# RetNet attention and a SwiGLU block on one core: the first pair in chunks of 128, the sixth weight asked for later, and three more seven-product sets in tile two

## The chip, the core and the metric

The kernel runs on one core of a Trainium2 chip. The metric is device time in microseconds. The engines are TensorE (PE, with its weight loads shown apart as PEld), VectorE (DVE), ScalarE (ACT), GpSimd (POOL) and SyncE (SP, which here only issues transfers). ACT issues transfers too, on a queue of its own, and POOL a few.

## The reference

```python
# attention: q, k, v are (8, 8, 576, 64), float32
scores = q @ k^T / 8
gamma  = 1 - 2**(-5 - head)                       # one decay for each head
ret    = scores * gamma**(i - j)  where i >= j, else 0
x      = (ret @ v), heads side by side            # (8*576 tokens, 512)
# SwiGLU block, weights float64 in DRAM
g   = x @ w_gate                                  # 512 -> 1536
out = (silu(g) * (x @ w_val)) @ w_out             # 1536 -> 512
```

## The kernel before

**Attention** goes by pairs of heads: pair `i` is batch `i // 4`, heads `2p` and `2p + 1` of it, 32 pairs in all. It is computed in chunks: within a chunk scores are masked with a triangle of decays (`near`), across chunks a state of 64x64 a head is carried on. For a pair, `transposes` turns q and k so that head positions lie on partitions (the first four pairs on PE, against the identity, later ones on DVE), `keys` scales the keys for the states, `scores` and `new_states` are matmuls of 64x64, `masked` is the mask and the chain of state sums on DVE (`own`, `pairs`, `odd`, `evens`), `own_values` and `earlier_values` are the matmuls with v and with the states, and `to_x` writes the result into the activations `x`, which lie with features on partitions. One attention step, `tick(t)`, does the values of pair `t - 2`, the scores and states of pair `t - 1` and the transposes of pair `t`. Its DVE and ACT parts go into a list, `pieces`, and are issued a few at a time between other work (`part_on`, `go_on`).

**The weights** are float64 in DRAM, so each has 1 MB pieces (18 of them, in `order`), loaded by `load_w(m)` into three raw buffers and a fourth place, and turned into float32 in halves of 512 columns: `split(j)` on ACT (two instructions, L389 and L390) and `rounding(j)` on DVE (L406 and L407). When a second half has been split, the load of the next weight into the freed place is issued: from the sixth weight on (`m >= 5`) on ACT's queue, else on SP's. The load of the sixth weight is not issued there but put into a list, `held`, and taken out later.

**The tokens** are 4608. Tile one has 512 and is multiplied plainly: `up0(f)` is block `f` of 128 hidden features, gate and value, over four chunks `c` of 128 input features, then SiLU on ACT and the product on DVE; `down0` follows. While it runs, PE also works off attention pairs 4 to 11. The other four tiles have 1024 tokens each and use two nested levels of a seven-product scheme (Strassen's) in the up projection, and a 26-product scheme in the down projection (`down_step`).

**The up stage** of a 1024-token tile goes over 3 blocks of hidden features (`qd`) by 7 outer products (`SETS`, in the order 1, 2, 6, 7, 4, 5, 3). Each of these 21 sets is done either by seven inner products, which need sums of x blocks (`x_inner`, on POOL) and sums of weights (`w_inner`, on POOL), or plainly, as eight: `PLAIN` lists the plain ones, all in tile two (`n == 1`), where the sums are still being made. A slot is one product: two matmuls of 256 columns at L1186. A product is read out of its bank by DVE (`combine`, L1042) or ACT; four banks go round. A plain set reads each bank once for its two slots (set 5 twice), a set of seven reads each product. `finish` is SiLU on ACT (L1200) and a product on DVE or POOL (L1201).

In tile two the weight sums are made on POOL, used, and stored to DRAM (`store`, on SP) for the later tiles. `later(at, f)` puts an instruction ahead of slot `at`; `begins[k]` is the first slot of set `k`.

**Order.** From L1425 on the order on every engine is as written in the code. Before it the loads are issued in this order: on SP the small tables (`tab`, 64 columns), then pair by pair q, k, v, pairs 0 to 3, the large tables between pairs 2 and 3, then the weights; pairs 0 and 1 have one head on SP's queue and one on ACT's. Then `tick(0)` to `tick(5)` do pairs 0 to 3, with the first weights and the first blocks of `up0` between them; then `plan` runs the rest of tile one.

Of the kernel before, what the change touches and what calls it, by code (L numbers as in the profile page):

```python
# [22 lines left out]
def tables(gamma, scale, L):  # L23
# [15 lines left out]
             both(g[:, None] ** L), both(g[:, None] ** (2 * L)), pieces, runs, both(scale * g[:, None] ** at),  # L39
# [70 lines left out]
PLAIN = {(1, qd, o) for qd in range(3) for o in (1, 2, 4, 5, 3) if qd == 0 and o == 1 or o in (4, 5, 3)}  # L110
# [21 lines left out]
def kernel(  # L132
# [121 lines left out]
    def load(i):  # L254
# [6 lines left out]
        if i < HP:  # L261
# [11 lines left out]
            for h in heads:  # L273
                queues[i % 2].dma_start(out=blocks(t)[:, h % 2], in_=v[b, h, 0:CW].rearrange("(c p) d -> p c d", p=P))
# [35 lines left out]
    NCOL = 6 * H + 4 * HP  # L310
    nc.sync.dma_start(out=tab[:, 0:NCOL], in_=decays[:, 0:NCOL])
    load(0)
    load(1)
    ident = const.tile([P, P], F32, name="ident")
    make_identity(nc, ident)
    nc.scalar.activation(out=io[:, 0:1], in_=ident[:, 0:1], func=AF.Silu)
    inv, key = tab[:, 0:H], tab[:, H : 2 * H]
    step = tab[:, 2 * H : 2 * H + 2 * HP]
    piece = tab[:, 2 * H + 2 * HP : 2 * H + 4 * HP]
    run = tab[:, 2 * H + 4 * HP : NCOL]  # L320
# [11 lines left out]
    even_heads, odd_heads = slice(0, H, 2), slice(1, H, 2)  # L332
    for rows in half:
        decay(slice(0, H), slice(0, H), rows)

    load(2)
    nc.sync.dma_start(out=tab[:, NCOL:], in_=decays[:, NCOL:])
    load(3)
# [20 lines left out]
    def load_w(m, parts=range(2)):  # L359
# [8 lines left out]
        if i < NUP:  # L368
            for cols in [ts(2 * f + n, D) for f in parts for n in range(2)] if m <= RAWS else [slice(0, 2 * P)]:
                queue.dma_start(out=dst[:, :, cols], in_=src[:, :, cols])  # L370
        else:
            queue.dma_start(out=dst.rearrange("p (f c) n -> p f (c n)", f=2), in_=src)
# [38 lines left out]
    for f in range(2):  # L411
        for m in range(2):
            load_w(m, (f,))
# [30 lines left out]
    def vector(i):  # L444

        return i == 0

    def transposes(i):
# [6 lines left out]
        copy = nc.scalar.copy if i else nc.vector.tensor_copy  # L455
        if i < HP:

            mine = (bankC, bankE) if i + 1 == HP else (bankB, bankA)
            parts = [(kT, kn, mine[0]), (qT, qk, mine[1])]
            if i == 0:  # L460
                parts.reverse()

            def turn(t, src, bank):
                for c in range(NFULL):
                    to = bank[:, c : 4 * P : NFULL] if t is qT and scaled(i) else bank[:, ts(c, P)]
                    nc.tensor.transpose(to, src[:, ts(c, P)], ident)

            def put(t, _, bank):
                if i or t is qT:
                    copy(t[:, 0:CW], bank)  # L470
                else:
                    copy(t[:, 0 : CW // 2], bank[:, 0 : CW // 2])
                    nc.scalar.copy(t[:, CW // 2 : CW], bank[:, CW // 2 :])

            if i + 1 == HP:
                for part in parts:
                    turn(*part)
                pieces = [lambda part=part: put(*part) for part in parts]
            else:
                for part in parts:  # L480
                    turn(*part)
                    put(*part)
# [13 lines left out]
        def keys():  # L496
# [5 lines left out]
            for hl, rows, at in parts:  # L502
                scale = key[rows, 2 * p + hl : 2 * p + hl + 1]
                if vector(i) or 1 < i < HP:
                    (nc.vector if vector(i) else nc.gpsimd).tensor_scalar(out=at, in0=at, scalar1=scale, scalar2=None, op0=ALU.mult)
# [5 lines left out]
        return [keys] + pieces  # L511
# [64 lines left out]
    def masked(i):  # L576
# [6 lines left out]
        def copies():  # L583
            (nc.vector.tensor_copy if vector(i + 1) else nc.scalar.copy)(out=even, in_=z[:, 0])
# [151 lines left out]

    def tick(t, lo=HP, hi=NP, spread=False, then=None):
        go_on(len(pieces))
        if hi == HP:

            def new_pair():
                scores(t - 1, True)
# [827 lines left out]
```

## Time and profile before

| | |
|---|---|
| median of three runs | 1018.75 us (1016.43 to 1019.09) |
| profiled execution | 1014.55 us, of which the span 1012.8 |
| PE | 1000.9 us busy, 99% of the span |
| DVE | 710.9 us, 70% |
| POOL | 561.8 us, 55% |
| ACT | 286.7 us, 28% |
| DMA | 194.38 MB, mean 192 GB/s |
| first matmul | 4.63 us after the span's start |
| first matmul of `up0` | 24.11 us |
| tile two's up stage | 172.2 to 319.4 us |

The profile is of one execution. Its times count from the span's start. "Busy" for PE is the time in which a matmul is under way; matmuls overlap, so the distance from start to start tells more than a duration. A group of PE with "x4" counts records: a float32 matmul has two of them, a transpose one. "A <- B" in a list of waits says that A was idle and that B's end released it.

### The profile page before, as it was taken

To read this page: it belongs to the slowest core of one execution; us is meant where nothing else is said; L and a number is where in the kernel's file an instruction comes from. 1 tells how busy PE (TensorE), PEld (TensorE's weight loads), DVE (VectorE), ACT (ScalarE), POOL (GpSimd) and SP (SyncE) were. 2 spreads that over 40 slices of the span, in tenths; PEclk is the share of its full clock that TensorE was granted. 3 is DMA by queue.
4 is the path that set the end of the run, shared out by engine and by line. 5 is a ranking of instruction groups with operands and counts; after the bars stand their busy time and mean duration, and the time that the engine had idled before them with its cause. 6 is when DMAs were issued, how large, how long until landed. Compare 5 with 4: busy or idle time off the path is not lost.

```text
span 1012.8 us, 21319 instructions
## 1 busy us (share of the span) xinstructions
PE 1000.9 (99%) x8336; PEld 825.5 (82%) x8336; DVE 710.9 (70%) x1206; ACT 286.7 (28%) x636; POOL 561.8 (55%) x589
## 2 busy tenths in 40 slices
PE   6999999999999999999999999999999999999998
PEld 5655555888888888888888888888888888888887
DVE  4488887677875766977777678866575767566645
ACT  4565522132423312133422202233220012232110
POOL 3400359979375228575564157746672586566514
PEclk9999999999999999999999999999999999999999
DMA  9999866967587787647677777434454554445553
GB/s 245 261 288 272 192 216 234 264 193 214 138 238 207 217 231 193 198 156 196 184 202 206 198 179 217 154 133 159 161 172 141 154 189 147 148 155 180 182 159 102
DMA packets 278892, 194.38 MB, mean 192 GB/s; under 512 B 212552, under 2 KB 246088, under 8 KB 278792
## 3 DMA queue, kind: packets, MB, share of 16 engines
q1 hardware_dynamic: 251464, 94.70, 36.7%
q10 hardware_dynamic: 26688, 97.92, 29.1%
q8 instruction: 66, 1.08, 0.5%
q0 software_dynamic: 640, 0.39, 0.2%
q14 instruction: 34, 0.28, 0.1%
HBM read 154.04 MB, written 38.93 MB: 191 GB/s over the span
## 4 chain that ended last, share of the span: by engine, by line
PE 94%; DVE 2%; DMA 1%; POOL 1%; SPq 0%; issue 0%; ACT 0%; DVEq 0%; ACTq 0%; POOLq 0%
PE bankB L1186 12%; PE bankC L1186 11%; PE bankA L1186 11%; PE bankE L1186 11%; PE bankB L1392 7%; PE bankC L1392 7%; PE bankE L1392 6%; PE bankA L1392 6%; PE outer L532 2%; PE bankE L853 2%; PE bankA L853 2%; PE outer L1186 2%; PE inner L1186 2%; PE bankB L853 2%; PE outer L559 2%; PE bankC L853 2%
## 5 line engine op out<-in xcount | busy, mean ns | idle before, releaser
L1042 POOL TENSOR_TENSOR rest<-rest 128x512 f32<-128x512 f32 (+1 forms) x139 | 148.0, 1076 | 159.9 <-DVE rest L1042 112.5
L1201 POOL TENSOR_TENSOR arena<-rest,io 128x256 f32<-128x256 f32 x168 | 123.9, 750 | 89.4 <-ACT io L1200 88.9
L1200 ACT ACTIVATE io<-rest 128x256 f32<-128x256 f32 x192 | 79.3, 417 | 200.0 <-DVE rest L1042 140.0
L1186 PE MATMUL bankB<-rest,arena 128*128 128x256 f32 x448 | 114.5, 380 | 0.0
L1042 DVE TENSOR_TENSOR rest<-bankB,rest 128x512 f32<-128x512 f32 x116 | 78.5, 685 | 40.5 <-PE bankB L1186 28.5
L1186 PE MATMUL bankC<-rest,arena 128*128 128x256 f32 x416 | 106.3, 380 | 0.0
L1186 PE MATMUL bankA<-rest,arena 128*128 128x256 f32 x412 | 104.8, 379 | 0.0
L1042 DVE TENSOR_TENSOR rest<-bankA,rest 128x512 f32<-128x512 f32 x111 | 75.2, 685 | 40.8 <-PE bankA L1186 19.3
L1042 DVE TENSOR_TENSOR rest<-bankC,rest 128x512 f32<-128x512 f32 x110 | 74.5, 683 | 38.0 <-PE bankC L1186 23.4
L1042 DVE TENSOR_TENSOR rest<-bankE,rest 128x512 f32<-128x512 f32 x106 | 71.7, 684 | 36.2 <-PE bankE L1186 17.6
L1186 PE MATMUL bankE<-rest,arena 128*128 128x256 f32 x372 | 94.9, 380 | 0.3 <-DVE rest L1042 0.3
L1186 PEld LDWEIGHTS bankB<-rest,arena 128*128 128x128 f32 x448 | 84.7, 190 | 11.9 <-DVE rest L1042 0.2
L1186 PEld LDWEIGHTS bankC<-rest,arena 128*128 128x128 f32 x416 | 78.5, 190 | 11.4 <-DVE rest L1042 0.8
L1186 PEld LDWEIGHTS bankA<-rest,arena 128*128 128x128 f32 x412 | 78.1, 190 | 10.9 <-DVE rest L1042 0.2
L1186 PEld LDWEIGHTS bankE<-rest,arena 128*128 128x128 f32 x372 | 70.3, 190 | 10.4 <-DVE rest L1042 0.8
L1042 POOL TENSOR_TENSOR arena<-arena 128x256 f32<-128x256 f32 (+1 forms) x76 | 70.3, 947 | 11.1 <-PE bankC L1186 9.0
L886 POOL TENSOR_TENSOR rest<-rest 128x512 f32<-128x512 f32 x21 | 28.5, 1377 | 72.1 <-DVE rest L407 58.5
L1392 PE MATMUL bankB<-arena 128*128 128x256 f32 x264 | 61.0, 381 | 0.0
L1392 PE MATMUL bankE<-arena 128*128 128x256 f32 x264 | 60.8, 380 | 0.0
L1392 PEld LDWEIGHTS bankE<-arena 128*128 128x128 f32 x264 | 50.0, 190 | 6.9
L1392 PEld LDWEIGHTS bankB<-arena 128*128 128x128 f32 x264 | 49.8, 190 | 6.9
L1392 PE MATMUL bankC<-arena 128*128 128x256 f32 x240 | 55.2, 379 | 0.0
(270 smaller groups left out, 1876.0 us busy)
## 6 DMA issues: line engine op xcount, KB each, us to landing
arena<-up ACTq DMA_DIRECT2D x63, 896.0 KB, 4.6
arena<-dn ACTq DMA_DIRECT2D x65, 384.0 KB, 3.1
arena<-dn SPq DMA_DIRECT2D x39, 384.0 KB, 3.1
out_dram<-rest SPq DMA_DIRECT2D x31, 256.0 KB, 3.4
qk<-in_q_dram SPq DMA_DIRECT2D x108, 72.0 KB, 3.1
qk<-in_k_dram SPq DMA_DIRECT2D x108, 72.0 KB, 3.4
dn<-rest SPq DMA_DIRECT2D x26, 256.0 KB, 2.8
up<-arena SPq DMA_DIRECT2D x13, 512.0 KB, 5.6
```

The lines of the kernel that those rows point to most:

```text
L532: m = nc.tensor.matmul(value(i, hl, c), s["v"][rows, at], ret[rows, c % 2 if whole(i) else hl, c // 2], start=start, stop=start, skip_grou ...
L559: nc.tensor.matmul(xr[half[hl]] if c + 1 == NC else value(i, hl, c), state[half[hl], c, :], s["qT"][half[hl], ts(c, L)], start=False, stop ...
L853: nc.tensor.matmul(bank, w, xs[0][:, c, :], start=(c == 0), stop=(c == HP - 1))
L886: eng.tensor_tensor(out=dst, in0=srcs[0], in1=srcs[1], op=ALU.add if op[0] == "add" else ALU.subtract)
L1042: eng.tensor_tensor(out=out, in0=a, in1=b, op=ALU.add if sign > 0 else ALU.subtract)
L1186: m = nc.tensor.matmul(b[:, g * TB : (g + 1) * TB], w[:, g], x, start=(opens and g == 0), stop=True, skip_group_check=True)
L1200: nc.scalar.activation(out=s, in_=src[:, 0:TB], func=AF.Silu)
L1201: (nc.vector if busy and o != 2 and qd + 1 < NQ else nc.gpsimd).tensor_tensor(out=hid[:, qd, 2 * H + h, 2 * T + t], in0=src[:, TB : 2 * TB ...
L1392: nc.tensor.matmul(b[:, m * TB : (m + 1) * TB], lhs[:, qd, ts(m, P)], w[:, qd], start=(opens and qd == 0 and m == 0), stop=(qd == NQ - 1), ...
```

## The change

1. **Loads.** q and k of pairs 0 and 1 are asked for first, their v after them (`load` now returns a function that asks for v). The small tables grow by 132 columns to 196 and go behind the first head's k. Pair 2 follows, then the first halves of weights 0 and 1, pair 3, the other halves, and weights 2 and 3, these in one transfer each instead of four. The large tables go behind the load of pair 4.
2. **Pair 0** is done in chunks of 128 tokens (`first_scores`, `first_states`, `first_own`, `first_out`), with tables of its own, and q is scaled as it is copied out of its bank. Matmuls whose result is not used are put in front of and between its transposes.
3. **The start** is written out step by step instead of by `tick`. Weight halves are rounded, and parts of `up0(0)` done, between pairs 1, 2 and 3.
4. **The sixth weight.** `held` is worked off after `to_x(3)` instead of before `split(4)`.
5. **Pair 4's first attention step** goes behind `up0(2)`.
6. **Three sets** of tile two, (1, 3), (2, 4) and (2, 3) as (`qd`, set), are no longer in `PLAIN`. The x sums of sets 3 and 4 are made on POOL for them, into places of their own.
7. **Attention steps in tile two**: five in the up stage, at slots 56, 70, 84, 97 and 111, and five in the down stage at steps 1, 5, 10, 14 and 19. Before there were six, spread evenly from slot 56 on, and four. Three fetches of down operands are asked for 36, 39 and 43 slots after the third block's start, instead of 36, 38 and 40.

```diff
-PLAIN = {(1, qd, o) for qd in range(3) for o in (1, 2, 4, 5, 3) if qd == 0 and o == 1 or o in (4, 5, 3)}
+PLAIN = {(1, qd, o) for qd in range(3) for o in (1, 2, 4, 5, 3) if qd == 0 and o == 1 or o in (4, 5, 3)} - {(1, 1, 3), (1, 2, 4), (1, 2, 3)}
...
-            for cols in [ts(2 * f + n, D) for f in parts for n in range(2)] if m <= RAWS else [slice(0, 2 * P)]:
+            for cols in [ts(2 * f + n, D) for f in parts for n in range(2)] if m < 2 else [slice(0, 2 * P)]:
...
-    for f in range(2):
-        for m in range(2):
-            load_w(m, (f,))
+    for m in range(2):
+        load_w(m, (0,))
+    load(3)()
+    for m in range(2):
+        load_w(m, (1,))
     load_w(2)
     load_w(3)
...
+    def first_scores():
...
+        for _ in range(2):
+            nc.tensor.matmul(bankB[0:D, 0:D], ident[0:D, 0:D], ident[0:D, 0:D], start=True, stop=True)
+        for src, bank, idle in ((None, None, 6), (qk, bankE, 2), (kn, bankC, 1)):
+            for c in range(NFULL if bank else 0):
+                nc.tensor.transpose(bank[:, ts(c, P)], src[:, ts(c, P)], ident)
+            for _ in range(idle):
+                nc.tensor.matmul(bankB[:, 0:P], ident, ident, start=True, stop=True)
...
+        for c, hl in first:
+            nc.tensor.matmul(inner[:, hl, ts(c, P)], kT[half[hl], ts(c, P)], qT[half[hl], ts(c, P)],
+                             start=True, stop=True, skip_group_check=True)
...
+        if n == 1:
+            new[4] = [w_up[:, NQ - 1, 0, h, k, :] for h, k in ((0, 0), (1, 0), (0, 1))]
+            new[3] = [xs[2][:, h, TW - TB :] for h in range(3)]
...
-            for o, at in {7: 6, 1: 22}.items():
+            second, third = begins[len(SETS)], begins[2 * len(SETS)]
+            for o, at in {7: 6, 1: 22, 3: second + 38, 4: third + 17}.items():
...
-    for t in range(HP + 2):
-        tick(t, 0, HP)
-
-        if t == 3:
-            load(HP)
-        for j in {3: (1,), 5: (4, 5)}.get(t, ()):
-            rounding(j)
+    scale_run(1)
+    first_scores()
+    scale_run(2)
+    turn_pair(1)
+    first_states()
+    first_own()
+    new_pair(1)
+    turn_pair(2)
+    first_out()
+    split(0)
+    rounding(0, False)
+    scale_run(3)
+    new_pair(2)
+    own_values(1)
+    split(1)
...
+    up0(0, [0], [0])
+    earlier_values(1)
+    to_x(1)[0]()
+    put = transposes(3)
+    rounding(1, False)
+    for f in put:
+        f()
+    up0(0, [1], [0])
+    up0(0, [0], [1])
+    split(2)
+    own_values(2)
+    earlier_values(2)
+    up0(0, [1], [1])
+    to_x(2)[0]()
+    rounding(2)
+    rounding(3, False)
+    new_pair(3)
+    load(HP)
+    nc.sync.dma_start(out=tab[:, NCOL:], in_=decays[:, NCOL:])
+    split(4)
+    up0(1, range(2))
+    own_values(3)
+    earlier_values(3)
+    to_x(3)[0]()
+    while held:
+        held.pop()()
+    rounding(4)
+    rounding(5, False)
     for c in range(2, HP):
         for f in range(2):
             up0(f, [c])
+    split(6)
     load(HP + 1)
```

## The prediction

> **What bounds the kernel now.** I read the page's engine totals first, then TensorE's waits, the chain that ended last, and the timeline of the first 40 us and of tile two.
>
> ```profile
> PE 1000.9 (99%) x8336; PEld 825.5 (82%) x8336; DVE 710.9 (70%) x1206; ACT 286.7 (28%) x636; POOL 561.8 (55%) x589
> ```
>
> Of the 1012.8 us span TensorE (PE) idles 11.9. Its waits show where:
>
> ```profile
> PE bankA L466 <- DMA qk<-in_q_dram: 4.6, 1, 4.6
> PE outer L532 <- ACT rest L389: 1.0, 1, 1.0
> PE inner L573 <- ACT rest L470: 0.7, 1, 0.7
> PE inner L573 <- DVE kT L472: 0.5, 1, 0.5
> PE bankE L1186 <- DVE rest L1042: 0.3, 1, 0.3
> ```
>
> All but 0.3 or so lie before 34 us; from there PE runs without a gap to the end. So two things shorten this kernel: reaching that gapless run earlier, and having fewer matmuls in it. "Busy" hides a third loss, in PE's timeline (start, us, line, count):
>
> ```profile
> 9.67 1.12 PE L466 MATMUL bankB<-ident,kn 128*128 128x128 f32 x4
> 12.36 1.13 PE L573 MATMUL inner<-rest,kT 64*64 64x64 f32 x32 [0.72 <-ACT rest L470]
> 20.54 0.66 PE L466 MATMUL bankC<-ident,rest 128*128 128x128 f32 x4
> 27.74 0.69 PE L573 MATMUL inner<-rest,kT 64*64 64x64 f32 x32
> ```
>
> Four transposes take 0.90 from start to next start at 9.67 and 0.49 at 20.54; 32 score records 0.90 and 0.51. The rate doubles at 17.0, though the granted clock reads 1.00 in every stretch. Last, the chain up to the gapless run:
>
> ```profile
> 27.81 0.62 PE inner L573 x32
> 28.43 0.53 PE inner L543 x32
> ...
> 29.39 0.69 DVE rest L580
> 30.08 0.40 DVE rest L596
> 30.50 0.30 DVE rest L603
> ...
> 31.60 0.40 DVE rest L608
> ...
> 33.37 0.68 PE outer L559 x28
> 34.05 1.05 PE bankA L853 x2
> ```
>
> It is pair 3's scores, mask and states, then its last values, then the first matmul of chunk 2 of `up0`, at 34.05. Ahead of it DMA moves 220 to 340 GB/s from 2 us on without a pause, so the order of the loads matters.
>
> **The start, step by step.** I lay the new order out with the durations of these rows. By the ends of their packets in the trace, q of pair 0 lands at 4.6, k at 5.9, pair 2 by 13.1, pair 3 by 17.0, the halves of weights 0 and 1 at 18.9, 20.8, 22.8, 24.7 (1.9 each, 0.52 MB). In the new order the second table part (0.26 MB) leaves this stretch, the first grows by 0.07, and pair 3 (0.79 MB, 3 us) goes behind two halves: halves at 15.2 and 17.1, pair 3 at 20.1, the other two halves at 22.1 and 24.0, weight 2 at 27.8, weight 3 at 31 (estimates).
> - To 7.7: nothing is won. PE still waits for q (4.4) and k (5.7). The larger table is asked for third and lands near 6.5; DVE's product of q (0.69), the kT halves (0.42, 0.37) give scores at 7.7, before 7.62. The nine 128-column filler matmuls and two small ones take about 0.43 each at the slow rate (one of 256 columns takes 0.43 at the fast one), in time PE would wait; at most the one behind k's transposes costs 0.4.
> - Pair 0 by 128: scores 8 matmuls (0.85: 8 x half of 0.43, two side by side), states 8 (0.43), own 8 (0.85), earlier 6 (0.64), 2.8 where 64-token chunks take 2.4 fast but cost about 3.6 at the slow rate.
> - Pair 1: transposes to 10.1 (its q lands 7.2, POOL's L735, 1.04, ends 9.65 behind both `near` selects), ACT copies 0.6 each to 10.95, keys 0.9 to 11.85, states done 12.65 (before 15.1); its DVE mask and states (2.5) to 15.65.
> - `split(0)` on ACT waits for the half at 15.2, two at 0.6: 16.4; `rounding(0)` on DVE ends 17.05; the first `up0` matmul starts there, before 24.11.
> - Pair 2's mask and states queue behind it on DVE to 19.6, `rounding(1)` to 20.7. PE waits in order for pair 3's k (19.3), then two `up0` matmuls and pair 2's values to 23.2.
> - `split(2)` at 22.1 ends 23.4, the x copies 24.5, `split(3)` 25.7, `rounding(3)` 26.4, then pair 3's chain as above (2.3) to 28.7, values 0.65: chunk 2 starts at 29.4 to 29.9, before 34.05. **Minus 4.4** (middle). This end is set by DMA (22.1), then ACT and DVE in turn.
>
> The rate is the weak step. Before, PE was busy from 12.36 to 17.0 without a gap and then turned fast; after, fillers keep it busy from about 1.6 (ident is made by 1.5) to scores; 1.6 + 4.6 is 6.2, and with the gap at 4.3 I take it as fast by 8.5. The Trainium skill, "TensorE: Matmul & The Clock Gate", Part 1, says the array starts at half clock and is released by one free-running window of about 3.4 us of sustained work; the trace agrees with a turn after 4.6 us of it. The same page's Part 4 says transposes don't count as busy for this gate; here they do appear inside the 4.6 us (15.12 to 17.0), so the trace neither confirms nor clearly breaks it; by it the sum would be that of the first rival.
>
> **Weights and loads after it.** Weight 4 goes ahead of pair 4's load on SP: it landed at 48.3 (ACT waited 4.4 for it), now about 35. The sixth weight is asked for at about 30, as now (29.64, issue 0.41 on ACT), so about 4 us late against PE; it lands at about 39 (8.0 as now). `split(10)` on ACT waits for it, with the SiLU of block 2 queued behind; PE needs that bank at 51. Cost 0; without that cover, what it is later than 51. Weights 2 and 3 go as one issue instead of four: SP's issue time (3.1 and 4.1), hidden by transfers. Table part two, behind pair 4's load, is first read at 72.6. Pair 4's first attention step moves behind `up0(2)`: its transposes (1.5 on DVE) are needed by pair 4's states at 50 (54.9 now), load landed at about 43. Cost 0, covered by about 5 us.
>
> **Three sets.** A plain set is 8 slots, a seven-product set 7. A slot is two matmuls of 256 columns; the timeline has them 0.863 apart (218.81, 219.67, 220.54). 3 x 0.863 = **minus 2.6**, if nothing stalls:
> - DVE reads 7 products instead of 4 banks: 9 reads more, 0.60 from start to start, 5.4 us.
> - POOL gets eight sums of 128x256 (0.73): 5.8 us.
> - Attention step 17 (2.25 on PE, 4.0 on DVE) goes from the up stage to the down stage, PE time unchanged; DVE was 3.8 busy of 10 at 320. The others stand closer, 14 slots.
>
> DVE is the tight one:
>
> ```profile
> 240.00:250.00 10.00, 10.00 (x49) 8.79 (x48) 9.58 (x19) 0.99 (x3) 9.02 (x14) 1.00 0.57 198
> 260.00:270.00 10.00, 10.00 (x173) 8.75 (x171) 9.93 (x20) 4.37 (x10) 4.71 (x5) 1.00 0.13 22
> ```
>
> (columns: PE, PEld, DVE, ACT, POOL, clock, DMA). Slots 97 to 111 are the worst: 11 reads 6.6, eight products with SiLU at 0.34 2.7, one attention step with what is left over 4.7: 14.0 of 14 slots and one step on PE, 14.3. It fits, and a product may be read up to four slots late (3.4) before its bank is written again. POOL idles 9.0 at 256, where set 3's sums go (needed at 261), and for set 4 has 8 us of work against about 11. I take 0.3 for small stalls, as the one of 0.2 at 274. From 0 to 2.6 is open. The three later fetches go with the ring; they stood 9 us before use, now 7.
>
> **Sum.** -4.4 - 2.6 + 0.3 = -6.7. The profiled execution is 1014.55 (span 1012.8 and 1.75 around it), 4.2 below the median of the three runs (1018.75), so: 1007.9 for such a run, 1012.0 for a median.
>
> **Rivals.**
> 1. PE stays at the slow rate until about 14.6 (chance 0.13). Up to pair 1's states it then spends 0.85 + 0.9 + 0.43 + 0.85 + 0.8 more, less 0.9 of idle: 2.9, passed down the chain. -3.8: 1014.9. For: gaps at 4.3 and transposes among the fillers. Against: the turn at 17.0.
> 2. DMA keeps its pace and PE, 4 us ahead, waits for it between 45 and 75 (0.12): start gain given back, 1016.2. For: DMA share about 1.0 up to 110, k of pairs 5 and 6 landing (54.4, 72.4) only 5 to 7 us before their transposes. Against: SP has pauses waiting for buffers (73.7 to 77.2), so DMA can catch up, and weights are split 15 us before use.
> 3. Slower: DVE becomes the bound in tile two (0.07). Once it is over four slots late, each of its microseconds is PE's: the 5.4 of reads and steps 15 and 16 brought forward (8.0) make 13.4, so +6.7: 1025.5. For: 9.93 of 10 at 260. Against: the count above, and 2.6 idle at 252.
> 4. The sets don't give what they say, since sums come late on POOL and each set waits a slot (0.08): 1014.4.
>
> **Numbers.** My forecast has 0.60. About 0.3% (3.1 us) is what a measurement can tell. Below 1015.7: the forecast, rival 4, most of rival 1, a little of the spread of 2: 0.79. Within: the rest of 1, most of 2: 0.13. Above 1021.8: rival 3 and what I overlooked: 0.08. The range goes from 1008 (start -5.5, sets -2.6, and a run lower by the 2 that the three runs spread) to 1017 (rivals 1, 2, 4 in).
>
> **What would show it.** First `up0` at about 17 instead of 24.1 and chunk 2 near 29.6; transposes of pair 1 at 0.11 each; PE gapless after; 154 slots instead of 157 in tile two with the same 0.863; POOL's sums of set 3 before 261. It is wrong if PE waits for L389, L406 or loads between 30 and 75, if L1186 waits on DVE L1042 for over 1 us in total, or if chunk 2 starts later than 32.

## Result and the profile after

The changed kernel takes **1031.57 us** (median of four runs, 1029.3 to 1034.7) where the one before takes 1018.25 (1016.43 to 1019.09): ratio **1.0142**, interval 1.0117 to 1.0167. It is slower by 13; forecast were 1012.0 and a range that ended at 1017. The profiled execution took 1034.70, with a span of 1033.0, against 1014.55 and 1012.8 before. The spans differ by 20.2, and the readings below are made against that. The profile after is the slowest of its four executions and the one before is faster than all four beside it, so some 7 of the 20.2 us may be the spread between executions. Below, line 869 of the changed kernel is L853 of the one before, L1205 is L1186, L1058 is L1042, L1412 is L1392, L872 is L856.

The engine totals of the page after:

```profile
PE 1007.7 (98%) x8294; PEld 829.9 (80%) x8294; DVE 723.8 (70%) x1213; ACT 286.0 (28%) x636; POOL 566.5 (55%) x598
```

PE has 42 records fewer, and is busy 6.8 us longer. Its idle time is 25.3 (span less busy) where it was 11.9. The list of its waits after (us in total, times, longest):

```profile
PE bankB L1412 <- DMA arena<-dn: 5.8, 1, 5.8
PE bankA L869 <- ACT io L872: 4.8, 2, 3.6
PE bankA L1205 <- DVE rest L1058: 2.9, 1, 2.9
PE inner L558 <- issue: 2.0, 1, 2.0
PE bankB L732 <- POOL ident masks.py:199: 1.6, 1, 1.6
PE outer L552 <- DVE kT L477: 1.3, 1, 1.3
PE bankA L869 <- DVE arena L416: 0.9, 1, 0.9
```

Of the first four, only 0.3 at L1186 was there before. All but the fifth and the last stand behind 70 us, in three places: ahead of 130, near 275, near 405 (the last, at 18.39, is the first `up0` matmul). Why busy time grew although matmuls were taken out shows in the windows around the three long waits (PE, PEld, DVE, ACT, POOL, granted clock, DMA share, GB/s):

```profile
100.00:110.00 10.00, 6.42 (x13) 2.45 (x12) 6.50 (x13) 8.44 (x16) 0.00 (x0) 0.88 1.03 264
110.00:120.00 10.00, 10.00 (x154) 5.50 (x153) 8.53 (x17) 7.27 (x15) 1.37 (x1) 0.95 0.89 214
270.00:280.00 10.00, 6.17 (x56) 5.11 (x57) 7.75 (x14) 2.32 (x7) 2.88 (x3) 0.91 0.78 166
280.00:290.00 10.00, 10.00 (x119) 8.52 (x121) 8.27 (x17) 4.39 (x10) 6.28 (x7) 0.92 0.58 189
400.00:410.00 10.00, 4.21 (x13) 3.22 (x12) 0.69 (x1) 0.00 (x0) 3.88 (x4) 0.73 0.78 237
410.00:420.00 10.00, 10.00 (x44) 8.68 (x44) 6.60 (x9) 1.17 (x2) 6.44 (x6) 0.93 0.98 240
```

The clock, 1.00 elsewhere in tile two, is below it behind each wait. The missing shares times 10 us are 1.7, 1.7 and 3.4. Of the last, a part falls into the wait itself, which ends at 407.04:

```profile
404.60:407.00 2.40, 0.00 (x0) 0.00 (x0) 0.00 (x0) 0.00 (x0) 1.34 (x2) 0.50 0.97 344
407.00:411.30 4.30, 4.26 (x10) 3.49 (x11) 0.00 (x0) 0.00 (x0) 0.00 (x0) 0.50 0.96 246
```

So some 2.2 of the 3.4 lengthen matmuls, and 5.6 in all. With 13.4 of new idle time that is 19.0 of the 20.2; the rest, with what the sets save and the added matmuls cost, was not split.

By place (the same matmul in both traces; stage lengths in us): chunk 2 of `up0` starts at 32.05 instead of 33.98 (34.05 in the chain of the page before), block 2 at 39.03 instead of 40.95. From block 2 to the first down matmul of tile one it takes 90.06 instead of 80.86, so that this comes at 129.09 instead of 121.81. The down stage of tile one is 50.38 in both. Tile two's up stage takes 149.75 instead of 147.26, its down stage 87.80 instead of 77.17. After that the two traces run alike. So: start +7.3, up stage +2.5, down stage +10.6.

### The profile page after: what moved, and what is told of

Same layout as the page of the kernel before. It is cut to its first block, busy times and chain, and to the rows that moved or that the text cites. A ratio compares the mean times of both kernels' runs of the same rounds, so it can differ in the third digit from the quotient of the medians.

```text
span 1033.0 us, 21261 instructions
## 1 busy us (share of the span) xinstructions
PE 1007.7 (98%) x8294; PEld 829.9 (80%) x8294; DVE 723.8 (70%) x1213; ACT 286.0 (28%) x636; POOL 566.5 (55%) x598
## 4 chain that ended last, share of the span: by engine, by line
PE 91%; DMA 4%; DVE 2%; ACT 1%; issue 1%; ACTq 0%; SPq 0%; DVEq 0%
PE bankE L1205 12%; PE bankA L1205 11%; PE bankC L1205 11%; PE bankB L1205 11%; PE bankB L1412 7%; PE bankA L1412 7%; PE bankE L1412 7%; PE bankC L1412 6%; PE outer L517 2%; PE outer L1205 2%; PE inner L1205 2%; DMA v<-in_v_dram 2%; PE outer L544 1%; PE inner L558 1%; PE bankE L869 1%; PE bankA L869 1%
## 5 line engine op out<-in xcount | busy, mean ns | idle before, releaser
L1058 POOL TENSOR_TENSOR rest<-rest 128x512 f32<-128x512 f32 (+1 forms) x143 | 150.8, 1066 | 165.6 <-DVE rest L1058 117.7
L1205 PE MATMUL bankA<-rest,arena 128*128 128x256 f32 x432 | 111.1, 382 | 2.9 <-DVE rest L1058 2.9
L1058 DVE TENSOR_TENSOR rest<-bankB,rest 128x512 f32<-128x512 f32 x115 | 78.0, 686 | 50.1 <-PE bankB L1205 24.3
L1058 DVE TENSOR_TENSOR rest<-bankA,rest 128x512 f32<-128x512 f32 x122 | 82.6, 686 | 38.1 <-PE bankA L1205 19.3
L1205 PE MATMUL bankB<-rest,arena 128*128 128x256 f32 x404 | 103.7, 381 | 0.0
L1205 PE MATMUL bankE<-rest,arena 128*128 128x256 f32 x396 | 101.8, 381 | 0.0
L1205 PE MATMUL bankC<-rest,arena 128*128 128x256 f32 x392 | 100.2, 380 | 0.0
L1058 DVE TENSOR_TENSOR rest<-bankC,rest 128x512 f32<-128x512 f32 x110 | 74.5, 685 | 34.2 <-PE bankC L1205 20.4
L1058 DVE TENSOR_TENSOR rest<-bankE,rest 128x512 f32<-128x512 f32 x106 | 72.0, 685 | 36.3 <-PE bankE L1205 24.9
L1205 PEld LDWEIGHTS bankA<-rest,arena 128*128 128x128 f32 x432 | 82.5, 191 | 15.0 <-issue 3.9
L1205 PEld LDWEIGHTS bankB<-rest,arena 128*128 128x128 f32 x404 | 76.5, 191 | 10.9 <-DVE rest L1058 0.6
L1205 PEld LDWEIGHTS bankE<-rest,arena 128*128 128x128 f32 x396 | 74.9, 190 | 10.9 <-DVE rest L1058 0.9
L1205 PEld LDWEIGHTS bankC<-rest,arena 128*128 128x128 f32 x392 | 74.5, 190 | 10.4 <-issue 0.4
L1058 POOL TENSOR_TENSOR arena<-arena 128x256 f32<-128x256 f32 (+1 forms) x76 | 70.1, 945 | 13.6 <-PE bankC L1205 4.7
L1412 PE MATMUL bankB<-arena 128*128 128x256 f32 x264 | 63.1, 391 | 5.8 <-DMA arena<-dn 5.8
L1412 PEld LDWEIGHTS bankB<-arena 128*128 128x128 f32 x264 | 51.5, 196 | 13.5 <-issue 6.2
L1412 PE MATMUL bankA<-arena 128*128 128x256 f32 x264 | 61.0, 381 | 0.0
L1412 PEld LDWEIGHTS bankA<-arena 128*128 128x128 f32 x264 | 49.9, 190 | 6.8
L1412 PE MATMUL bankE<-arena 128*128 128x256 f32 x240 | 55.3, 380 | 0.0
```

Of the source, the lines that this page charges most:

```text
L1058: eng.tensor_tensor(out=out, in0=a, in1=b, op=ALU.add if sign > 0 else ALU.subtract)
L1205: m = nc.tensor.matmul(b[:, g * TB : (g + 1) * TB], w[:, g], x, start=(opens and g == 0), stop=True, skip_group_check=True)
L1412: nc.tensor.matmul(b[:, m * TB : (m + 1) * TB], lhs[:, qd, ts(m, P)], w[:, qd], start=(opens and qd == 0 and m == 0), stop=(qd == NQ - 1), ...
```

## Experiments

Each ratio is against the kernel before, timed beside it. Where a window, a wait or a stage is given without a fence, it is from the same views, of one profiled execution for each kernel. Two pairs of kernels below have the same start (the changed kernel and `start_alone`, `both_mended` and `start_mended`), and the stretch from block 2 to the first down matmul differs by 2.9 and 2.1 us within them. A difference of 3 us or less between two such stretches therefore says little.

### The parts alone

`start_alone` is the changed kernel with items 6 and 7 undone; `tile_two_alone` is the kernel before with items 6 and 7; `steps_alone` is the kernel before with item 7 alone:

```
-            merge((0.0, ticks(done, cut)), (0.5, ups))
+            places_of = [i - 8 * len(SETS) for i in (56, 70, 84, 97, 111)]
...
-            for i, f in reversed(list(zip((2, 7, 13, 19), ticks(cut, upto), strict=True))):
+            for i, f in reversed(list(zip((1, 5, 10, 14, 19), ticks(cut, upto), strict=True))):
```

> The start of the changed kernel (its parts 1 to 5) with tile two as it was before: same sets, same attention steps, same fetch slots. Theory S (start and tile two lose separately): in the changed kernel the first down projection starts at 129.1 us instead of 121.8, so 7.3 of the 20 lost are there; this kernel should start it near 129 and end 6 to 8 us later than the kernel before. Theory P (the losses of tile two come from the start: loads that are late there stay late): 15 to 20 us later than before. Forecast of the record (the start wins 4.4): 4 us faster.

> The kernel before with the changed tile two (three sets, attention steps and fetch slots moved), the start as before. Theory S: down projection of tile one starts at 121.8 as before, then the up stage of tile two is about 2.5 us longer and its down stage about 10.6, so 11 to 14 us slower than before. Theory P: 0 to 3 us slower or faster. Forecast of the record: 2.3 faster.

> The kernel before with only the attention steps of tile two and the three fetches moved, and the sets as before. If DVE's load in the up stage is lost to the sets (seven reads instead of four), the up stage has no stall here and shortens by the one step that leaves it, 2.2 us, to 145.0; if it is the crowding of the steps (14 slots apart), its stalls at the steps stay. If the 5.8 us wait of TensorE in the down stage comes from the fifth step's loads ahead of an operand's fetch on SP's queue, it is here too, and the down stage is about 10 us longer than the 77.2 of before.

Measured: 1.0066 (1.0044 to 1.0088), 1.0113 (1.0088 to 1.0137) and 1.0074 (1.0047 to 1.0101). **No part is a gain.** The start costs 6.7 us, moving the steps 7.5, and the sets on top of the moved steps about 4 (1.0113 less 1.0074). Start and tile two lose separately, as theory S had it: together they make 1.0179 where the whole has 1.0142, which the intervals allow. `steps_alone` shortens the up stage by 2.1 (145.16), as one step less should, and lengthens the down stage by 10.4 (87.55).

### The down stage: who holds the operands back

SyncE's queue in the changed kernel, around the fifth step (start, time taken by the issue):

```profile
392.86 9.04 SPq L298 DMA_DIRECT2D v<-in_v_dram  x2
401.94 0.55 SPq L301 DMA_DIRECT2D v<-in_v_dram  x1
402.59 0.41 SPq L1013 DMA_DIRECT2D arena<-dn  x1
```

The attention step that went to the down stage issues loads. One of them, v, stands 9.04 us in the queue, and the fetch of the last down operands stands behind it until 402.59; PE waits for that to 407.04 (5.8). In the program each DMA of SP's and ACT's queues carries one of eight semaphores in turn (100 to 107 in the trace), and is issued only when the last one on that semaphore has landed. The second half of the v transfer shares semaphore 107 with ACT's fetch of the next tile's up operands. That fetch goes out only at 396.97, because it needs a buffer that a late down step frees, and lands at 401.51; v is issued at 401.53. SyncE's list of waits names it too (the longest of seven is this one):

```profile
SPq L298 <- DMA arena<-up: 30.7, 7, 8.1
```

`steps_alone`, without sets and start, shows the same: v takes 9.04 at 383.81, the operands go out at 393.54, PE waits 5.63.

`steps_earlier` moves the second, third and fourth step of the down stage forward, so that the loads fall before that fetch:

```
-            for i, f in reversed(list(zip((1, 5, 10, 14, 19), ticks(cut, upto), strict=True))):
+            for i, f in reversed(list(zip((1, 4, 8, 12, 19), ticks(cut, upto), strict=True))):
```

> The kernel steps_alone with the five attention steps of tile two's down stage at 1, 4, 8, 12 and 19 instead of 1, 5, 10, 14 and 19. In steps_alone the last operands of the down stage stand on SP's queue behind the values of pair 21, whose transfer takes the semaphore that ScalarE's fetch of the next tile's first weights has to release (asked for at 388.0, landed at 392.5). Here all operands but the last stand ahead of that fetch. If that is the cause, the wait of 5.6 us goes and the down stage takes 79.4 us (77.2 and one step of 2.25) instead of 87.6, the whole 7 to 8 us less than steps_alone, as the kernel before. If it is the DMA traffic of five steps as such, the wait stays or moves, and the stage takes over 84.

Measured 1.0021 (1.0010 to 1.0032): the down stage takes 80.13, PE's wait is gone from the list, and in SP's queue the operands stand ahead of the loads:

```profile
378.38 1.38 SPq L997 DMA_DIRECT2D arena<-dn  x3
379.86 1.18 SPq L1402 DMA_DIRECT2D out_dram<-rest  x1
381.13 0.94 SPq L997 DMA_DIRECT2D arena<-dn  x2
382.24 0.47 SPq L1402 DMA_DIRECT2D out_dram<-rest  x1
386.56 2.86 SPq L282 DMA_DIRECT2D qk<-in_q_dram  x4
```

That settles the cause: by the ratios, 5.4 of the 7.5 us that item 7 cost were the place of a step's loads in a queue. The 2.1 that remain were not split further.

### The sets: why L1205 waits for L1058

With the steps of `steps_earlier`, two repairs for the wait of 2.9: `sets_pool` lets POOL make the products of set (1, 5); `sets_step104` has the attention steps at slots 104 and 118 instead of 97 and 111; `sets_both` has POOL's products and steps at 104 and 113.

```
# sets_pool, sets_both
-            (nc.vector if busy and o != 2 and qd + 1 < NQ else nc.gpsimd).tensor_tensor(
+            (nc.vector if busy and o != 2 and qd + 1 < NQ and (qd, o) != (1, 5) else nc.gpsimd).tensor_tensor(
# sets_step104 (sets_both: 104, 113)
-            places_of = [i - 8 * len(SETS) for i in (56, 70, 84, 97, 111)]
+            places_of = [i - 8 * len(SETS) for i in (56, 70, 84, 104, 118)]
```

> The kernel tile_two_alone with the same attention steps as steps_earlier, and the four products behind the SiLU of set 5, second block, made on POOL instead of DVE. In tile_two_alone TensorE waits 2.9 us at 271.2 for a read that stands on DVE behind such a product (1.5 us), which waits for a SiLU that stands on ScalarE behind an attention step's copies. Theory C (that chain, not DVE's load): the stall goes, and with it most of the slow clock behind it; the up stage takes 142 to 144 us instead of 148.1, and the whole is 3 to 5 us faster than steps_earlier. Rival B (DVE is full there, 1.6 us of products less change little): the stall stays over 1.5 us, and the up stage takes over 146.

> The kernel tile_two_alone with the steps of the down stage at 1, 4, 8, 12, 19 and, in the up stage, the attention step of slot 97 at 104 and that of 111 at 118 (all products on DVE again). Slot 97 is the first of the set (1, 3), which as a set of seven writes result 22 at slot 98, where the plain set wrote it at 104; the values of the set before it have to go through SiLU and product first, and with a step at 97 ScalarE makes that step's copies ahead of the SiLU. If that place is the cause, the stall of 2.1 to 2.9 us goes without any change of DVE's load, the up stage takes 142.3 to 143.5 us and the whole is 1 to 3 us faster than the kernel before. If DVE's load in these slots is the cause, a stall of 1 us or more comes at slots 104 to 112 instead, and the up stage takes over 144.5.

> The kernel sets_step104 with the products of set 5, second block, on POOL as in sets_pool, and the fifth attention step at slot 113 (118 gave late pieces at the end of the stage). Theory CB (two limits in turn: DVE's sum from slot 89 to 101, which sets_step104 showed without a pause of DVE, and the chain from an attention step's copies over SiLU and product to the read, which sets_pool showed with DVE idle): only with both taken away the stall at slot 100 goes; the up stage takes 142.3 to 143.5 us and the whole is 1 to 3 us faster than the kernel before. If it is still over 1 us, another cause is left.

Ratios: 1.0024 (1.0013 to 1.0036), 1.0089 (1.0073 to 1.0105), 1.0058 (1.0040 to 1.0076). Either repair alone leaves the wait, each for its own reason. In `sets_step104` PE waits 2.45 at 266.23 (and 1.82 at 316.40, behind the step at 118), and DVE, listed by time, has no pause (in these kernels L1189 is before's L1186):

```profile
258.45 1.28 DVE L1042 TENSOR_TENSOR rest<-bankA,rest 128x512 f32<-128x512 f32 x2
259.65 0.74 DVE L1204 TENSOR_TENSOR arena<-rest,io 128x256 f32<-128x256 f32 x1
260.31 0.77 DVE L492 STREAM_TRANSPOSE qT<-qk 128x576 f32<-128x576 f32 x1
...
262.18 1.11 DVE L1204 TENSOR_TENSOR arena<-rest,io 128x256 f32<-128x256 f32 x1
...
263.91 1.24 DVE L1042 TENSOR_TENSOR rest<-bankE,rest 128x512 f32<-128x512 f32 x2
265.08 0.40 DVE L1204 TENSOR_TENSOR arena<-rest,io 128x256 f32<-128x256 f32 x1
265.41 0.67 DVE L1042 TENSOR_TENSOR rest<-bankB,rest 128x512 f32<-128x512 f32 x1
```

From the first read of set (1, 5), at 256.53, to the end of the last one shown, which frees PE's bank, DVE takes 9.55 us for nine reads, four products and two transposes; PE's slots leave 7.8. A product costs 0.40 to 1.11 here. In `sets_pool` the up stage takes 144.90, between the two forecasts, and `steps_earlier` without the sets 145.26. PE waits 2.11 there, without a half clock behind it, and DVE idles, at the end of a chain:

```profile
264.94 1.13 ACT L626 COPY rest<-outer 128x256 f32<-128x256 f32 x3
265.97 0.41 ACT L1203 ACTIVATE io<-rest 128x256 f32<-128x256 f32 x1
266.47 0.72 POOL L1204 TENSOR_TENSOR arena<-rest,io 128x256 f32<-128x256 f32 x1 [3.83 <-ACT io L1203]
267.22 0.69 DVE L1042 TENSOR_TENSOR rest<-bankA,rest 128x512 f32<-128x512 f32 x1 [2.43 <-POOL arena L1204]
267.97 1.13 PE L1189 MATMUL bankA<-rest,arena 128*128 128x256 f32 x4 [2.11 <-DVE rest L1042]
```

A result of set (1, 5) is written over by set (1, 3), in a seven-product set six slots earlier than in a plain one. So its SiLU and product must be done first, and ACT copies the attention step's values ahead of them. In `sets_both`, with both removed, that wait is 0.31:

```profile
265.75 1.13 PE L1189 MATMUL bankA<-rest,arena 128*128 128x256 f32 x4 [0.31 <-DVE rest L1042]
281.22 1.06 PE L543 MATMUL inner<-v,kn 64*64 64x64 f32 x32 [1.99 <-issue]
```

Yet a new one of 1.99, for "issue", came at 281.22, with a stretch at half clock behind it (granted 0.83 over 280 to 290: 1.7 us). The up stage is 147.30; less 1.99 and 1.7 it is 143.6, against 147.26 before. Three sets and one step less would have made 142.4. By such subtraction (144.90 less 2.11 is 142.8 in `sets_pool`, against 145.26 with the steps alone) the sets are worth about 2 us, but no run shows it: each version spent it on a wait.

`sets_alone` and `sets_alone_pool` are the kernel before with item 6 alone, the second with POOL's products too:

> The kernel before with only the three sets done by seven products (their x sums on POOL), attention steps and fetch slots as before (steps at slots 56, 72, 89, 105, 121, 138). Forecast of the record for this part: 2.6 less in the up stage, 144.7 us, and the whole 2.3 faster. If DVE's sum from slot 89 to 101 decides (some 9.5 us of its work in the 7.8 that TensorE leaves), a stall of 1.5 to 3 us stands at slot 100, with the lower clock behind it, and the up stage takes 146.5 to 149.

> The kernel sets_alone with the four products of set 5, second block, on POOL. There is no attention step at slot 97 here and DVE has 1.6 to 2.7 us less, so by the two limits that sets_both showed no stall over 0.5 us at slot 100 is left, the up stage takes 144.5 to 145.3 us, and the whole is 1.5 to 2.6 us faster than the kernel before.

They gave 1.0164 (1.0147 to 1.0181) and 1.0117 (1.0098 to 1.0137). Both compute something else than the reference, so these are no times of the change: with the fetches at their old slots the third one, ahead of slot 144, lands on the weight sum that set (2, 4) still reads. Only the second's profile is read. Its up stage is 157.68, with a wait of 7.48 for that operand, to 318.5. Until the wait it took 137.05, where 144 slots of 0.863 and six attention steps of 2.1 make 136.9: up to there the sets kept the pitch. The moved fetch slots thus belong to item 6, not to the steps.

### The start

The first two undo one piece of the start each. `load4_early` is the changed kernel with pair 4 asked for before `split(2)`; `early_sixth` is `start_alone` with the sixth weight asked for before `split(4)`, as before the change.

```
# load4_early: ahead of split(2), no longer ahead of the large tables
+    load(HP)
     split(2)
...
-    load(HP)
# early_sixth: ahead of split(4), no longer behind to_x(3)
+    while held:
+        held.pop()()
     split(4)
...
-    while held:
-        held.pop()()
```

> The changed kernel with the load of pair 4 put ahead of the request for weight 4, in program order and on SP's queue (before the third half is split). Theory L (the loads of pairs 4 to 7 come late since a transfer is asked for only when the one eight places ahead of it has landed, and pair 4's stand behind weights 2, 3 and 4, of 1 MB each): pair 4's k lands 3 to 6 us earlier than 39 us, ScalarE's waits for k (5.7 and 8.1 us) shrink, and the down projection of tile one starts by 125 us instead of 129.1. Rival D (the DMA engines are full, whatever the order): it moves by less than 1 us, as weight 4 is late instead.

> The kernel start_alone with the sixth weight asked for ahead of the fifth half's split, as before, not behind the values of pair 3. The prediction gave this delay a cost of 0: by that, no change from start_alone (down projection of tile one starts at 126.1). If asking late is what the start loses by, it starts by 122.

Measured 1.0134 (1.0113 to 1.0154) and 1.0041 (1.0019 to 1.0062). From block 2 to the first down matmul of tile one: 85.83 instead of 90.06, and 83.76 instead of 87.20 in `start_alone`. By these profiles the pieces cost 4.2 and 3.4, little more than the 2.9 by which two executions of one start differ. By the times neither is shown: 1.0134 against 1.0142 and 1.0041 against 1.0066, with intervals that overlap. (`early_sixth` ran from 1014.12 to 1023.78, and its profile is of the slowest execution.) What goes wrong in the changed kernel shows in SP's queue; the last two lines are the kernel before:

```profile
24.68 8.61 SPq L290 DMA_DIRECT2D qk<-in_q_dram  x4
33.33 8.10 SPq L290 DMA_DIRECT2D qk<-in_k_dram  x4
...
43.97 3.63 SPq L1482 DMA_DIRECT2D tab<-decays  x1
...
27.95 4.07 SPq L282 DMA_DIRECT2D qk<-in_q_dram  x4
32.07 4.93 SPq L282 DMA_DIRECT2D qk<-in_k_dram  x4
```

Pair 4's q and k issues take twice as long as before. SyncE's waits name no weight for them: the issues themselves last longer, and why is not shown. The landings show what they stand behind: weight 4, asked for just ahead of them on this queue, lands at 35.9, the first of the q transfers at 36.4, and the two parts of k at 48.4 and 49.4 instead of 42.3 and 43.9. Later keys come late as well, and the ACT instruction that scales them holds up all that is queued on ACT:

```profile
99.24 0.96 ACT L492 ACTIVATE kn<-kn,tab 128x256 f32<-128x256 f32 x2 [8.05 <-DMA kn<-in_k_dram]
100.11 0.65 ACT L398 ACTIVATE rest<-rest 128x512 f32<-128x512 f32 x1
...
105.84 0.59 ACT L872 ACTIVATE io<-bankA 128x512 f32<-128x512 f32 x1
```

Before, the same instruction ran at 89.85 without a wait:

```profile
89.85 0.96 ACT L507 ACTIVATE kn<-kn,tab 128x256 f32<-128x256 f32 x2
```

Here the eight instructions of four splits and two requests follow first, then the SiLU that empties PE's bank; PE waits 3.58 to 106.48. The wait of 1.24 at 71.84 has the same form (5.68 for a key). In `load4_early` both are gone, and one of 2.09 stands at 55.07, behind a scaling of keys.

The question left was whether the order of requests is at fault, or PE being 2 to 4 us early against a DMA that is busy all the time (rival 2 of the prediction). Six kernels took it on: `old_loads`, with all loads asked for in the order of before; `step4_early`, `start_alone` with pair 4's first step at its old place; `start_mended`, with the sixth weight, pair 4's load and its step at their old places; `start_quarters`, that with weights 2 and 3 in quarters again; `tables_pool`, `start_alone` with the large tables on POOL's queue; `start_late`, `start_alone` with 43 matmuls of no use ahead of block 2.

```
# old_loads (from early_sixth)
+    nc.sync.dma_start(out=tab[:, NCOL:], in_=decays[:, NCOL:])
+    load(3)()                     # both ahead of the weights; load(HP) ahead of split(2)
# old_loads, start_quarters
-  ... if m < 2 else [slice(0, 2 * P)]:
+  ... if m <= RAWS else [slice(0, 2 * P)]:
# step4_early, start_mended (the latter with load(HP) ahead of split(2))
+    plan.insert(1, lambda: tick(HP, HP, FIRST))
# tables_pool
-    nc.sync.dma_start(out=tab[:, NCOL:], in_=decays[:, NCOL:])
+    nc.gpsimd.dma_start(out=tab[:, NCOL:], in_=decays[:, NCOL:])
# start_late, before split(6)
+    for _ in range(43):
+        nc.tensor.matmul(inner[0:D, 0, 0:D], ident[0:D, 0:D], ident[0:D, 0:D], start=True, stop=True)
```

> The kernel start_alone with all loads asked for in the order of the kernel before (pair 3 and the large tables ahead of the weights, weights 2 and 3 in four transfers each, pair 4 ahead of weight 4, the sixth weight early), the arithmetic of the new start kept. Theory L (order of the loads): the two stalls of TensorE at 71.8 (1.4 us) and 105.8 (3.0 us, with a lower clock behind it) go, and the down projection of tile one starts at 119 to 122, no later than before (121.8). Rival D (the DMA engines are busy without a pause from 2 to 110 us whatever the order, so TensorE, which is early, waits for them): stalls of 2 us and more stay somewhere between 45 and 115, and it starts at 121 to 126.

> The kernel start_alone with pair 4's first attention step back at its old place, behind the first two halves of block 2's rounding instead of behind block 2. With pair 4's k landing at 39 us and the step's transposes ahead of roundings on DVE, this alone should be no better than start_alone if the loads are late (block 2 to the first down projection 87 us, or longer), and 83 or less if the step's new place is what the start loses by.

> The kernel start_alone with three things as before: pair 4 is asked for ahead of weight 4, the sixth weight ahead of the fifth half's split, and pair 4's first attention step stands at its old place. The order of the first loads (q and k first, pair 3 behind two weight halves, weights 2 and 3 whole) stays new. Theory L (what is asked for behind weights 2 to 5 comes late): block 2 starts near 39 us and the first down projection 81 to 82 us later, near 120.5, so 1 to 2 us faster than the kernel before. Rival D (TensorE 2 us early outruns the DMA engines whatever the order): the stalls stay, 84 us or more between the two.

> The kernel start_mended with weights 2 and 3 asked for in four transfers each, as before. In start_mended ScalarE's request of the seventh weight waits 6.5 us for pair 4's last q transfer, which was asked for only when the last half of weights 0 and 1 had landed; here that q waits for quarters of weight 2. Theory W (eight transfers may be open, counted over both queues, so a whole weight of 1 MB among them holds back what is asked for behind it): the stalls of 2.4 and 2.0 us at 41 and 58 go or halve, block 2 to the first down projection takes 81 to 83 us instead of 84.7. Rival D: stays at 84 or more.

> The kernel start_alone with the large tables asked for on POOL's queue instead of SP's, so that pair 5's load stands 3.6 us nearer on SP's and ScalarE's request of the ninth weight (56.5 us) doesn't wait for the tables to land. Theory W: pair 5's k lands 2 to 4 us earlier than 64.6, the stall at 71.8 (1.4 us) goes, and block 2 to the first down projection takes 83 to 86 us instead of 87.2. Rival D (bytes decide): no change over 1 us.

> The kernel start_alone with 43 matmuls of 64x64, whose result is not used, ahead of block 2 of the up projection: TensorE comes to block 2 about 6.2 us later (near 45.1 us instead of 38.9), at full clock, and nothing else is moved. Rival D (TensorE is early and outruns loads that come at their own pace): the stalls behind it go, block 2 to the first down projection takes 81 to 82 us instead of 87.2, and the delay costs at most 1 us in the end. Theory W (loads asked for in an order that makes TensorE wait whenever it comes): the stalls stay, 85 us or more, and the whole is 4 to 6 us slower than start_alone.

| kernel | ratio (interval) | block 2 at | to first down matmul | waits of PE over 0.9 us in that stretch |
|---|---|---|---|---|
| `start_alone` | 1.0066 (1.0044-1.0088) | 38.86 | 87.20 | 1.38 at 71.8, 3.02 at 105.8 |
| `old_loads` | 1.0086 (1.0066-1.0107) | 45.21 | 81.33 | none |
| `step4_early` | 1.0061 (1.0045-1.0077) | 39.69 | 84.92 | 1.92 at 52.2 |
| `start_mended` | 1.0073 (1.0038-1.0108) | 41.36 | 84.70 | 1.97 at 58.6 |
| `start_quarters` | 1.0062 (1.0041-1.0083) | 39.37 | 89.17 | 1.46, 2.65, 1.89 |
| `tables_pool` | 1.0046 (1.0028-1.0063) | 39.20 | 85.37 | 2.18 at 55.4, 1.83 at 105.9 |
| `start_late` | 1.0130 (1.0113-1.0146) | 44.21 | 88.69 | 4.59 at 97.2 ("issue") |

Each repair removes or shortens the wait that it was made for, and another comes up: `tables_pool` ends the one at 71.8, `step4_early` those of L872; then `tables_pool` waits for v at 55.4, `step4_early` for a rounded weight at 52.2. Weights 2 and 3 in quarters (`start_quarters`) did not shorten the stretch; that expectation missed. With the old order (`old_loads`) the first `up0` itself comes at 23.32, after a wait of 6.3 with the clock at 0.50:

```profile
20.00:25.00 5.00, 1.69 (x2) 0.50 (x2) 2.75 (x7) 2.70 (x5) 0.00 (x0) 0.50 1.01 292
25.00:30.00 5.00, 4.79 (x69) 2.89 (x71) 2.19 (x6) 3.31 (x7) 1.82 (x2) 0.86 1.05 296
```

`start_late` has no wait for a load left, which speaks for "PE is early", but its stretch holds another one and the half clock behind it:

```profile
97.21 0.90 PE L558 MATMUL inner<-qT,kT 64*64 64x64 f32 x18 [4.59 <-issue]
```

The half clock (6.83 us from 96.24 on) costs 2.9 behind the wait's end. Less 4.59 and 2.9, 88.69 is 81.2, near the 80.86 of before. On the other side `start_mended` shows the order at work where DMA wasn't full: its share is 0.64 over 38 to 42 us, while ACT waits to request a weight, with a SiLU behind it, for 6.51. The request carries the semaphore of pair 4's last q transfer, which landed at 39.81:

```profile
39.89 0.45 ACTq L379 DMA_DIRECT2D rest<-in_moe_w_gate_dram  x1
40.71 0.60 ACT L872 ACTIVATE io<-bankA 128x512 f32<-128x512 f32 x1 [6.51 <-DMA qk<-in_q_dram]
```

So both are there, and which has the larger share **stays open**. What the table does show: every kernel that reached block 2 between 38.8 and 41.4 with a changed order of requests took 1.7 to 9.2 us more than before for the stretch behind it (`both_mended` below least, the change itself most); the two that came at 44 or later wait for no load there.

`both_mended` is the changed kernel with `start_mended`'s and `sets_step104`'s edits:

> The changed kernel with what start_mended and sets_step104 put back. If both hold and their gains add, 2 to 5 us faster than the kernel before (-1 to -2 of the start, -1 to -3 of tile two); if the start's loads still come late, up to 5 us slower.

Measured 1.0090 (1.0074 to 1.0106), stretch 82.57, up stage 150.74, down stage 80.15: by the ratios 5 us better than the change, still 9 slower than before, where at most 5 were expected. No version tried beat the kernel before.

## Why the prediction was wrong, step by step

**To 7.7 and the rate: mechanism right.** Ahead of 4.89 a filler takes 0.45 from start to start (six in 2.72). The four transposes at 4.89 take 0.59 to the next start, and the two fillers at 5.48 0.44, half as much each; so do the four transposes at 5.92:

```profile
4.89 0.75 PE L735 MATMUL bankE<-ident,qk 128*128 128x128 f32 x4
5.48 0.61 PE L737 MATMUL bankB<-ident 128*128 128x128 f32 x4
5.92 0.60 PE L735 MATMUL bankC<-ident,kn 128*128 128x128 f32 x4
```

PE is fast from about 5, some 3.4 after the first filler at 1.55, not 4.6 as worked out. Scores come at 7.04 instead of 7.7. Rival 1 is out.

**The start, minus 4.4: size off.** Chunk 2 came at 32.05 (1.9 won), not 29.4 to 29.9. The four halves landed at 16.3, 18.1, 22.8 and 25.6 instead of 15.2, 17.1, 22.1 and 24.0, so the first `up0` came at 18.39 instead of 17.05, and `rounding(3)` ended 1.5 late. Then "values 0.65" counted only the values from the states: PE, without a wait over 0.2 from 23.40 on, came to pair 3's own values at 30.57, behind `up0(1)`, and needed 1.48 from there to chunk 2. The term was summed from a DMA pace without slack, and PE's own work at the end was left out.

**"Weights and loads after it ... Cost 0": this step failed**, by the most: the stretch behind block 2 grew by 9.2. In `start_alone`, with the same start, it grew by 6.3. The load of pair 4 was put at "about 43" and its keys landed at 48.4 and 49.4, since it stood behind weights on SP's queue. Later keys came late too, and ACT, waiting for them (5.68 and 8.05), held back the SiLUs that free PE's banks. The sixth weight was asked for at 32.17 and landed at 42.1, where 30 and 39 were put. It was priced by its own split and block 2's SiLU, for which PE indeed did not wait, not by later requests. Which of late requests and an early PE has the larger share stays open, as said above. Rival 2 (0.12) named the direction; it took the loss to be the start's gain at most (1016.2), and it was 6.3 to 9.2 where that gain was put at 4.4.

**Three sets, minus 2.6 and 0.3 for stalls: failed in size.** The up stage was to be 142.4, and 142.7 with the 0.3, and took 149.75: waits of 2.9 and 1.3, 0.9 for "issue", and 1.7 of half clock. Rival 3 (0.07) named the place, L1205 on L1058. The claim "Slots 97 to 111 are the worst", with 14.0 of work in 14.3, chose a window that began too late: the queue builds from slot 89, where set (1, 5) still has eight reads. Products on DVE were put at 0.34 each; in `sets_step104` they take 0.40 to 1.11. And a product "up to four slots late" isn't so where the same result is overwritten by the next set's product.

**Attention step 17 "goes from the up stage to the down stage, PE time unchanged": failed.** PE's time is unchanged; its DMAs were not followed past the fetches on SP's queue. 5.8 of waiting, and 2.2 of half clock behind it, make 8.0 of the 8.4 by which the down stage is over the forecast.

**What no step had: the clock.** Each long wait was priced at its length. The traces show the granted clock at 0.50 for 3.41 or 6.83 us around or behind waits of 1.52 to 6.3. Each 3.41 us in which PE works costs 1.7 on top; in the wait itself it costs nothing, as at 407. The Trainium skill, "TensorE: Matmul & The Clock Gate", Part 1, gives a free-running window of 3413 ns after which an idle array goes to half rate; the trace agrees with the length. The same page, "Why this matters for your kernels", asks for no idle gaps over about 3 us; here, past the first 30 us, waits of 1.92, 1.97, 2.09, 2.38, 2.45 and 2.65 already cost a window, while others of 1.89, 2.08, 2.11, 2.18 and 2.40 did not. Of three of 1.99 two did, and one of 1.52 did (`old_loads`, with 0.60 more right behind), but none up to 1.49. On that the measurement decides.

The forecast's three misses by stage, 11.7 (7.3 measured, minus 4.4 expected), 7.0 and 8.4, make 27.1, which brings minus 6.7 to the 20.4 found at the end of tile two.

## What to carry to other kernels

When a step is moved, lay out its DMA requests in the order of their queues and of the semaphores that they take in turn, and see for each which transfer must land before it is issued and what stands behind it, compute on the same engine included. In a kernel whose matrix engine runs without a gap, a new wait of about 2 us may cost 1.7 more in clock, as it did in six kernels here (1.92 to 2.38), so an edit that saves 2 us must create none. Where an engine is 9.9 of 10 busy, take every start of the window for the count, not the one that looks busiest.

## What the hardware showed beyond that

PE waited several times for "issue" alone: 2.0 at 128.71 in the changed kernel, 1.99 at 123.66 in `early_sixth`, 1.99 at 281.22 in `sets_both`, 1.89 in `start_quarters`, 4.59 at 97.21 in `start_late`. In each of them a packet of the queue that the page lists as q8, "instruction" (66 packets in the whole span), ends within the wait, 1.4 to 1.9 us ahead of its end. That PE waited for its own instructions is argued from this, not shown; such waits came and went with edits elsewhere in the program, and three of the repairs above met one.
